# Thresholded attention and a gated MLP on one core: the tanh form of Gelu as one ScalarE function, with a new step order

## The chip, the cores and the metric

The kernel runs on one core of a Trainium2 chip, as one program. The metric is the device time of one execution in microseconds. Three runs of the kernel before gave 970.08, 971.67 and 973.45 us, so its median is 971.67 us. The engines are named as the profile names them: PE (TensorE), PEld (its weight loads), DVE (VectorE), ACT (ScalarE), POOL (GpSimd), SP (SyncE, which issues all DMAs here).

## The reference

Attention over 8 batches, 8 heads, 576 positions and head size 64, with a threshold below each row's maximum, and then a gated MLP over the concatenated heads:

```python
scores = scale * (q @ k.T)
keep = scores >= max(scores, axis=-1) - tau
attn = where(keep, exp(scores - max), 0); attn /= sum(attn) + 1e-9
x = heads_side_by_side(attn @ v)              # (8, 576, 512)
h = x @ w_in                                  # (8, 576, 1024)
h = 0.5 * h * (1 + tanh(c * (h + 0.044715 * h**3)))
u, v = h[..., :512], h[..., 512:]
v_n = (v - mean(v)) / sqrt(var(v) + 1e-6) * g_ln
gated = u * (w_sg @ v_n + b_sg[:, None])
out = x + gated @ w_out
```

The line with tanh is the one that the change touches.

## The kernel before, in words

**The attention part** (`attention`, lines 429 to 834) works on 32 pairs of heads. Each pair has nine tiles of 128 rows by 576 columns of scores. A tile goes through a fixed chain: PE makes the scores in PSUM (step `s`, line 558; line 533 for the first four pairs), DVE takes the negated row maximum (`nm`, line 567), POOL makes the threshold (`thr`, line 573), ACT takes the exponential from PSUM with the maximum as bias (`exp`, line 594), and DVE selects against the threshold, multiplies and sums (`stt`, line 601). Then the tile is turned. From the fifth pair on, tiles of both heads go out to DRAM and back by DMA (`move`, line 609, and `fetch`, line 618) and are turned in blocks by DVE (`turn32`, line 625); the rest is transposed on PE and copied out by ACT (lines 738 and 753). PE multiplies with the values (line 764), DVE scales (line 773), and ACT and POOL split the result into a rounded part `xh` and a remainder `xl`. The q and k of a pair are loaded, split and placed by further DMAs; these stand on lines 453 to 500.

**The MLP part** (`moe`, lines 874 to 1090) works on one batch at a time, between the attention tiles of the next batch, and on the last batch alone. Per batch there are five `v` units (four of 128 rows by 512 columns and one of 64 rows, whose accumulator is first folded into the tile `vt`), eight `u` units (128 by 288 in the first seven batches, 128 by 256 or 320 in the last), eight `y` units (the gate) and eight `o` units (the output). Products of all units are issued at line 866 in pieces of at most four matmuls. Each of the 13 `v` and `u` units of a batch ends with `gelu2` (line 838), which puts four steps into the plan:

- `msq`, line 845, ACT: Square of the accumulator into a buffer `gt`, scaled;
- `stt1`, line 852, DVE: (buffer + c) times the accumulator, back into the buffer;
- `tanh`, line 854, ACT: Tanh of the buffer, in place;
- `stt2`, line 849, DVE: (buffer + 1) times the accumulator, into the unit's own tile.

The accumulator stays in its PSUM bank through all four. The result is twice the Gelu, and later steps allow for that: the variance of `v` is normalised with 4e-6 in place of 1e-6 (line 946), and the gate multiplies by 0.5 (`mg`, line 1016). After a `v` unit follow DVE's statistics (lines 939 and 942), POOL's variance, power and shift (lines 946 to 954), ACT's normalisation (line 958), and the gain and the split into two parts (lines 961 to 976, POOL and ACT).

**What sets the order.** Every step is put into a plan of 5584 entries. A table, `ORDER`, is a permutation of the plan that is stored compressed; `issue` calls the steps in that order, and each engine's queue is then worked through in that order. A second table, `FIRST_BANKS`, names the PSUM bank of each request. SP issues all 1062 DMAs in the order of their steps.

Of the kernel before, what the change touches and what calls it, by code (L numbers as in the profile page):

```python
# [14 lines left out]
F32 = mybir.dt.float32  # L15
# [3 lines left out]
ALU = mybir.AluOpType  # L19
# [3 lines left out]
P = 128  # L23
# [6 lines left out]
GELU_C = 0.7978845608028654  # L30
GELU_A = 0.044715
# [40 lines left out]
    "Q1K)KJP+id|vru7<#@HhSsQ!r0;>%;RoHM2GQtq49^7D-65{9^H4Y7Vo>Pts#`$*o^)(U6i&Wya~Rs$tsV@`0Ozuv=<iiQk6TgDzw+SRnidN>GZ^|{ME"
    "nMrs{0zI0j$?Nw{UsR^14*lwbbz$xUvAY9?g@=5;{o}ci{BN@(-`@jrX67`{9R0FPwxIb|(D%^+CuuGSyx&G3U<TqJl1V_JQqq)V##QT3`M_!K?Ojcjw"
    "tRFT$w5$=ajAmAPjPf3SCv*7g22)q(MXaq*lxiNewj8oWf$*qVA=Qy1cbk%rylJJz;XdX$*cmSjr3DqWg|t1QVuOGH@YUIOsh`bCRE7O9=`hw=vtzImr"
    "S`kTCilcFC*%hoCUK3q5%7^hk0r9mh8s{`MJ@A&dfnSJGz0G}^eajtWuTWk!lYE%9gctjdLByc_0m;OryZ?BR0@&1`Ga#{f3mHfBDj9G8G2A9QNpKY)#"
    "(Y_78nm*egz@%U>N6mltRKHjNo1Xyl!ruD^S{7L_<AvWy(E5%aBvu|AQQ5<}YSUF%yPb$TW*h$rz{-y|xOwX%ThF`dNX-bed*vq@)05YNE!W`c0$96Xu"
    "bh!<<@M(BB;YF|;f){R{NO=(Vn2YBlExvEdguz_)#32bwEIrJcix{JGx7$V)FvI(ZoLdwlc4xg>U~RSS2G_7^)u&BI0pqE76SY+Bne7SM(HmFcd2!ZD~"
    "*MMHx~BsJrNdBWjvpOuy07xH3r;qM63K&Evoc_GF^k4f6&FRCOh|3lFC;to|3DF=yhQEbx52ALr5y9iL%s3H`a>*ApI7qm8_G_yN#7q(bjnD|0d)Q05h"
    "$<AgB6gSa?{(@RFUSVU|udV`UPUaQ5+Zgjx>j{CsQhJ<h-dTY}GtsrRIVSqs0aY3+GaXV>2AU*t||1^!kK98d&Hu>HoT+Y8gJccfLTqaMbO{#lxMq?Rm"
    "t_)c^)R)0)N<)7W^Az$p3zPA5mNaPy~SD<;wT`9=#Ku+$1gr=Z#p;EBk?4O61#Q<JBtqm_6C0-ba75yJ{>cAg+Njfv-u;j|f-#EP!2qlk`p8V~^h#k+J"  # L80
    "h2f_Fq8cHfF<=kCB)nn({4(WE$JPW>_sdd;yB!4VFSMqi(ir>NNVt^RPrMh&N8Hyq%R4>BOmnv1Xb$cIE?#`cv^yWxtp+~iwdte4r?dzlzGlGDF?5oPI"
    "0uk!*4g(#x4RkAr5EkFA@OCe?o%JywO>xVBs<RZEpX#CZV0FmU!aXU*ymzw(zfY%q$6fM(fX<3sW|zzs2u_M(SKZc<>QZknq^plHzm;fx(h@z7@mO-SX"
    "BU#Pez{r2!8~viNz2VmNyj6@-O-PnOeDem95*JaHBDM9#p`D3(0(0Z-?x>Q0W9|n(a{}4~5QW<#T`^J}LXu<JaA`(zL=@{jXuEyeSO$9aEhTqokFG4m<"
    "X~G3=;TDl3O`Fwa<N<W<*uyZ8^5o6=DhL;;i~PeuHEh_XX=^2{uKu5A*Jcw5-AImb&wOjt_z3_4tf_0jO|YFGz+&3hugdw$#*Pax}(3Hx(e){W3CU%qn"
    "tBjbhd1AnyRX?1v*J?rHE`pA;irOmf?8a*Iz(ziB<I8&lG>v<hn>r;<Tt|)Z>xoB_Z`3I6#n|3-Ihxt`L(plS?XdfC4r={(S^ZUfY+sTC|Y+CqX=JC?o"
    "+AvYLn)E8v!gmu4Uw>rDi4KSRLw}8`afVsI(2^QrDvS9;N*N-p20S};TATJbj5txyw_rk5XYBvKJpn8G-1oh@6hs9Bl<*~8$K3C-PcGsOl5Ew(h<!l~d"
    "YbwG&0V`J*<`6`N-Zhpb@T6ag_9uw$49De4#BQYO*o=;Xp=X;al5-&fAY06&!6E{I7D%LO<wPqvZ4f+R+G1NL2uAQRc`#FSZGfAr3XNVyg_+`^zi$*yv"
    "Vb0@ZNbi|2WlnUJAiEfn7d=6b_A{Py`Om_1?Cq*WpVixt~>FM7|}ly#DIq6BVa39fI$nvCo87ZGJ5BAy{uL{Oy^a8}rE<^vFLH;9hK@gproa+>x6R*@U"
    "+acFC%9Hn)^(r1U&%2fWA8M$}=y0gWIEjrbGTV1Q<@<EEmRpiZU!5PG6lqtI}8s<3#v6l@Ku4~l(?msGq9clh}L-0X%o<hTIg_Dgy7KJYB2E8hO%d0_N"
# [53 lines left out]
def tile_threshold_attention_gated_mlp(  # L143
# [691 lines left out]

    xh_of, xl_of = {}, {}

    def gelu2(put, end, acc_of, tile_of, nm_):

        t, tag = {}, slot("gt", 2)  # L840

# [5 lines left out]
        def gate():  # L847
            t["h"] = tile_of()
            nc.vector.scalar_tensor_tensor(t["h"], t["tmp"], 1.0, t["acc"], ALU.add, ALU.mult)  # L849
# [317 lines left out]
```

## Time and profile before

| | |
|---|---|
| median of three runs | 971.67 us |
| the profiled execution | 971.18 us, of which the span from first to last instruction is 969.4 us |
| granted TensorE clock, mean | 0.993 |
| PE, DVE, ACT, POOL busy | 889.2, 856.8, 560.1, 563.9 us |
| DMA queue 1, share of 16 engines over the span | 76.0% (212.40 MB) |
| ACT table loads | 1 |

Busy time is the time in which an instruction of the engine runs. Matmuls are pipelined and their ends are modelled, so a busy PE need not be a PE at its peak: a 128x288 matmul is shown as about 0.30 us while the next may start 0.13 us after it. The first 95 us hold the weights and the first pairs, the stretch from 95 to 865 us runs attention and MLP side by side, and from about 865 us on the last batch's MLP is alone.

### The profile page before, as it was taken

What the parts mean: (1) busy time and instruction counts of PE and PEld (TensorE: products, weight loads), DVE (VectorE), ACT (ScalarE), POOL (GpSimd) and SP (SyncE); (2) the same over time, 40 slices, a digit from 0 to 9 for tenths busy, and PEclk for the clock granted to TensorE, in tenths of its full rate; (3) what the DMA queues carried; (4) which work ended last, traced back from release to release, by engine and by line L of the source; (5) the groups of instructions that cost most, each with busy time, mean ns of one, the idle gap of its engine ahead of it and who ended that gap; (6) DMA issues with size and microseconds to landing.
All of it is one profiled execution on the core that took longest, in us unless ns stands there. A gap on an engine that the chain in (4) does not pass through costs nothing. (4 is left out here: it accounts for less than half of the span.)

```text
span 969.4 us, 18918 instructions
## 1 busy us (share of the span) xinstructions
PE 889.2 (92%) x5958; PEld 728.3 (75%) x5958; DVE 856.8 (88%) x1623; ACT 560.1 (58%) x1179; POOL 563.9 (58%) x997
## 2 busy tenths in 40 slices
PE   8999999889799898999889998999989999799998
PEld 4656777766688777987768777787778777598897
DVE  8999999999998899999999899998999899976541
ACT  6897764546654566544665456554565545554562
POOL 5765655546644566536754557646575456565287
PEclk9999999999999999999999999999999999999999
DMA  6533889999899897899878988899888898764001
GB/s 239 172 110 87 225 227 260 273 281 283 221 271 263 230 289 210 257 279 267 250 232 243 274 250 252 224 266 267 259 238 244 247 272 259 205 191 119 14 1 62
DMA packets 205388, 213.61 MB, mean 220 GB/s; under 512 B 22132, under 2 KB 141159, under 8 KB 205288
## 3 DMA queue, kind: packets, MB, share of 16 engines
q1 hardware_dynamic: 205288, 212.40, 76.0%
q8 instruction: 47, 0.77, 0.3%
q14 instruction: 53, 0.43, 0.1%
HBM read 103.03 MB, written 66.18 MB: 175 GB/s over the span
## 5 line engine op out<-in xcount | busy, mean ns | idle before, releaser
L594 ACT ACTIVATE p<-all_banks,nm 128x576 f32<-128x576 f32 x256 | 186.4, 740 | 160.6 <-DVE nm L567 142.3
L625 DVE STREAM_TRANSPOSE pt<-m 128x512 f32<-128x512 f32 x216 | 244.5, 1141 | 10.6 <-DMA m<-d 10.1
L567 DVE TENSOR_REDUCE nm<-all_banks 128x1 f32<-128x576 f32 x288 | 207.5, 746 | 20.8 <-PE all_banks L558 14.5
L601 DVE SCALAR_TENSOR_TENSOR p<-all_banks,nm,p 128x576 f32<-128x576 f32 x256 | 203.9, 807 | 12.5 <-ACT p L594 5.6
L558 PE MATMUL all_banks<-ks,qst 128*128 128x288 f32 x560 | 161.5, 320 | 23.9 <-DVE p L601 9.5
L573 POOL TENSOR_TENSOR nm<-columns,nm 128x1 f32<-128x1 f32 x288 | 54.0, 193 | 209.1 <-DVE nm L567 179.3
L764 PE MATMUL all_banks<-pt,rv 128*64 128x320 f32 (+1 forms) x1024 | 139.8, 412 | 12.7 <-DVE pt L625 10.5
L558 PEld LDWEIGHTS all_banks<-ks,qst 128*128 128x128 f32 x560 | 103.5, 191 | 47.1 <-DVE p L601 19.7
L558 PE MATMUL all_banks<-kl,qz 128*128 128x288 f32 x448 | 125.3, 296 | 1.8 <-POOL kl L466 1.7
L764 PEld LDWEIGHTS all_banks<-pt,rv 128*64 128x64 f32 x1024 | 71.0, 136 | 63.0 <-issue 9.9
L866 PE MATMUL all_banks<-wsh,z 128*128 128x288 f32 (+2 forms) x512 | 114.4, 299 | 1.4 <-DVE uu L1016 0.9
L866 PEld LDWEIGHTS all_banks<-wsh,z 128*128 128x128 f32 x512 | 85.1, 188 | 3.5 <-DVE uu L1016 1.3
L558 PEld LDWEIGHTS all_banks<-kl,qz 128*128 128x128 f32 x448 | 84.8, 189 | 3.0 <-POOL kl L466 2.9
L866 PE MATMUL all_banks<-xh,wih 128*128 128x288 f32 (+2 forms) x256 | 78.1, 307 | 7.0 <-ACT tt L753 3.0
L866 PE MATMUL all_banks<-gh,woh 128*128 128x288 f32 (+2 forms) x256 | 76.5, 302 | 1.7 <-DVE p L601 1.3
L866 PE MATMUL all_banks<-xl,wih 128*128 128x288 f32 (+2 forms) x256 | 77.2, 303 | 0.0
L866 PE MATMUL all_banks<-xh,wil 128*128 128x288 f32 (+2 forms) x256 | 76.5, 300 | 0.0
L866 PE MATMUL all_banks<-gh,wol 128*128 128x288 f32 (+2 forms) x256 | 75.5, 298 | 0.0
L866 PE MATMUL all_banks<-wsl,z 128*128 128x288 f32 (+2 forms) x256 | 75.3, 297 | 0.0
L866 PE MATMUL all_banks<-gl,woh 128*128 128x288 f32 (+1 forms) x240 | 71.7, 301 | 0.1
L866 PE MATMUL all_banks<-wih,xh 128*128 128x512 f32 x160 | 65.3, 410 | 2.7 <-DVE pm L601 2.1
L264 PE MATMUL all_banks<-ident_r,p 128*128 128x128 f32 x288 | 57.7, 284 | 10.2 <-DVE p L601 7.4
(146 smaller groups left out, 2138.0 us busy)
## 6 DMA issues: line engine op xcount, KB each, us to landing
d<-p SPq DMA_DIRECT2D x216, 256.0 KB
m<-d SPq DMA_DIRECT2D x216, 256.0 KB
rk<-in_kT SPq DMA_DIRECT2D x32, 320.0 KB
rv<-in_vP SPq DMA_DIRECT2D x32, 320.0 KB
ks<-khi SPq DMA_DIRECT2D x56, 160.0 KB
rq<-in_qT SPq DMA_DIRECT2D x31, 288.0 KB
qz<-qhi SPq DMA_DIRECT2D x56, 144.0 KB
qst<-rq SPq DMA_DIRECT2D x56, 144.0 KB
```

The costliest lines, as they stand in the source:

```text
L264: nc.tensor.transpose(out, x, ident_r.bitcast(F32))
L558: nc.tensor.matmul(sc[:, a, 0:HALF], w, x, start=(j == 0), stop=(j == len(terms) - 1))
L567: nc.vector.tensor_reduce(nmax, st["s", h, i][:, :, 0:HALF], AX.XY, ALU.max, negate=True)
L573: nc.gpsimd.tensor_tensor(thr, toff, st["nm", h, i], ALU.subtract)
L594: nc.scalar.activation(target(h, i), st["s", h, i][:, :, 0:HALF], AF.Exp, bias=st["nm", h, i])
L601: nc.vector.scalar_tensor_tensor(dst, st["s", h, i][:, :, 0:HALF], st["thr", h, i], dst, ALU.is_ge, ALU.mult, accum_out=st["l"][:, c:c + 1])
L625: nc.vector.transpose(unit(h, a)[:, :, j * P:(j + 1) * P].rearrange("p c (j a) -> p a c j", j=Q), st["m", h, i].rearrange("p (a k c) -> p ...
L764: nc.tensor.matmul(acc[h * D:(h + 1) * D, 0:w], st["v"][:, o:o + D], unit(h, a)[:, kt, 0:w] if kt < NM else tail_unit(a)[:, 0:w], start=(k ...
L866: nc.tensor.matmul(st["acc"], *term(j), start=(j == 0), stop=(j == n - 1))
```

## The change

`gelu2` with its four steps is replaced by `gelu` with one: ACT applies the function `Gelu_apprx_tanh` to the accumulator (or to `vt`) and writes the unit's tile. The buffers `gt` and `gtu` go. As the result is now the Gelu itself, the variance gets 1e-6 and the gate is a plain product.

```diff
-    def gelu2(put, end, acc_of, tile_of, nm_):
...
-            nc.scalar.activation(t["tmp"], t["acc"], AF.Square, scale=(GELU_C * GELU_A) ** 0.5)
...
-            nc.vector.scalar_tensor_tensor(t["h"], t["tmp"], 1.0, t["acc"], ALU.add, ALU.mult)
...
-        put("msq", end, square)
-        put("stt1", end, lambda: nc.vector.scalar_tensor_tensor(
-            t["tmp"], t["tmp"], GELU_C, t["acc"], ALU.add, ALU.mult))
-        put("tanh", end, lambda: nc.scalar.activation(t["tmp"], t["tmp"], AF.Tanh))
-        put("stt2", end, gate)
+    def gelu(put, end, acc_of, tile_of):
+        put("gelu", end, lambda: nc.scalar.activation(tile_of(), acc_of(), AF.Gelu_apprx_tanh))
...
-            gelu2(put, end, acc, new, f"{b}_{i}")
+            gelu(put, end, acc, new)
...
-                nc.gpsimd.tensor_scalar(t[:, 0:1], t[:, 7:8], 1.0, 4e-6, ALU.mult, ALU.add)
+                nc.gpsimd.tensor_scalar(t[:, 0:1], t[:, 7:8], 1.0, 1e-6, ALU.mult, ALU.add)
...
-            gelu2(put, time + spread, acc, new, f"u{b}_{p}_{d}")
+            gelu(put, time + spread, acc, new)
...
-                nc.vector.scalar_tensor_tensor(g, acc(), 0.5, g, ALU.mult, ALU.mult)
+                nc.vector.tensor_tensor(g, acc(), g, ALU.mult)
```

`ORDER` and `FIRST_BANKS` are new as a whole. The new table has 5272 entries. Decoded and laid over the plan, with the four steps of each unit replaced by one, it shows this:

- The stages stay where they were. When 72, 108, 144, 180, 216, 252 and 288 exponentials have been issued, both orders have issued 13, 25, 39, 52, 65, 78 and 91 of the units' Tanh or Gelu steps. The last 13 units of the 104 come after the last exponential in both.
- Steps that both orders share moved little: counted over the shared steps, nine in ten stand between 36 places earlier and 34 later, and the median is one place. This holds for SP's DMA steps as well, of which none is added or removed.
- On ACT's queue the 288 exponentials and the 104 Gelu steps form 84 runs of one function, so the function changes 83 times between the two. (Exponentials and Tanh steps formed 112 runs in the old order.) The last change is the one ahead of the last 13 Gelu steps.
- Between a tile's `nm` and its `stt`, DVE has a median of two other steps in both orders, and a mean of 2.75 in the old and 2.73 in the new. In the new order 69 of the 288 tiles have a change of function between their `nm` and their `stt`, and in 41 of them it is directly ahead of the tile's own exponential.

## Rows read from the trace of the kernel before

**Rows 1.** The page: busy time, share of the span and instructions of each engine.

```profile
PE 889.2 (92%) x5958; PEld 728.3 (75%) x5958; DVE 856.8 (88%) x1623; ACT 560.1 (58%) x1179; POOL 563.9 (58%) x997
```

**Rows 2.** Windows: stretch, PE, PEld, DVE, ACT, POOL busy (instructions), clock, DMA share, GB/s.

```profile
0.00:95.00 95.00, 86.74 (x540) 54.31 (x541) 87.73 (x204) 77.04 (x168) 59.98 (x122) 1.00 0.48 154
95.00:865.00 770.00, 703.74 (x4719) 584.19 (x4719) 719.87 (x1324) 433.83 (x902) 442.25 (x782) 0.99 0.88 250
865.00:969.00 104.00, 98.71 (x702) 89.85 (x700) 49.15 (x98) 49.25 (x110) 61.66 (x94) 1.00 0.20 59
```

**Rows 3.** Waits, whole span: who waited for whom, us in total, times, longest.

```profile
ACT p L594 <- DVE nm L567: 142.3, 106, 4.2
...
PEld all_banks L558 <- DVE p L601: 19.7, 31, 2.0
...
DVE uu L849 <- ACT gtu L854: 12.4, 10, 5.8
DVE pt L625 <- DMA m<-d: 10.1, 14, 2.1
...
DVE p L601 <- ACT p L594: 5.6, 15, 1.4
```

**Rows 4.** Windows, line 852 alone: stretch, DVE busy (instructions), clock, DMA.

```profile
95.00:865.00 770.00, 47.14 (x88) 0.99 0.88 250
```

**Rows 5.** Windows, line 849 alone: DVE busy.

```profile
95.00:865.00 770.00, 49.56 (x88) 0.99 0.88 250
```

**Rows 6.** Windows, line 854 alone: ACT busy.

```profile
95.00:865.00 770.00, 44.60 (x88) 0.99 0.88 250
```

**Rows 7.** Timeline of DVE near 118 us: start, us, engine, line, operation, tiles, shapes.

```profile
117.83 0.64 DVE L852 SCALAR_TENSOR_TENSOR gt<-gt,all_banks 128x512 f32<-128x512 f32 x1
118.39 0.41 DVE L355 TENSOR_TENSOR room<-all_banks,w 128x256 f32<-128x256 f32 x1
118.73 0.43 DVE L852 SCALAR_TENSOR_TENSOR gtu<-gtu,all_banks 128x288 f32<-128x288 f32 x1
119.09 0.20 DVE L652 RECIPROCAL ir<-l 128x9 f32<-128x9 f32 x1
```

**Rows 8.** Groups by shape: busy us, mean ns | idle before, releasers.

```profile
L594 ACT ACTIVATE p<-all_banks,nm 128x576 f32<-128x576 f32 x256 | 186.4, 740 | 160.6 <-DVE nm L567 142.3 <-DMA d<-p 5.3 <-issue 3.6
...
L845 ACT ACTIVATE gtu<-all_banks 128x288 f32<-128x288 f32 x56 | 22.5, 405 | 15.2 <-PE all_banks L866 11.6 <-DVE vv L849 3.2
...
L845 ACT ACTIVATE gt<-all_banks 128x512 f32<-128x512 f32 x32 | 18.8, 590 | 10.0 <-PE all_banks L866 10.0
...
L773 DVE TENSOR_TENSOR ir<-all_banks,ir 128x256 f32<-128x256 f32 x32 | 13.3, 416 | 1.7 <-PE all_banks L764 0.9 <-DMA d<-p 0.8
...
L1016 DVE SCALAR_TENSOR_TENSOR uu<-all_banks,uu 128x256 f32<-128x256 f32 x4 | 1.5, 415 | 0.8 <-PE all_banks L866 0.8
...
L307 ACT ACT_TABLE_LOAD x1 | 1.3, 1283 | 0.7 <-PEq L1148 0.7
```

**Rows 9.** Timeline of ACT, the first 10 us; in brackets the idle time before.

```profile
0.72 1.28 ACT L307 ACT_TABLE_LOAD   x1 [0.72 <-PEq L1148]
6.61 0.66 ACT L307 ACTIVATE room<-w 128x512 f32<-128x512 f32 x1 [4.61 <-DMA w<-in_w_in]
```

**Rows 10.** Windows with the columns of rows 2: the busiest 50 and 100 us of DMA.

```profile
195.00:245.00 50.00, 43.83 (x273) 32.05 (x273) 47.74 (x87) 28.65 (x56) 29.02 (x54) 1.00 0.98 283
200.00:300.00 100.00, 88.17 (x577) 70.02 (x576) 95.15 (x177) 56.96 (x117) 53.54 (x98) 0.98 0.91 261
```

**Rows 11.** The chain that ended last, 918 to 950 us: start, us, what.

```profile
923.41 0.53 ACT gt L854
923.96 0.70 DVE vv L849
...
942.23 0.37 ACT gtu L854
...
945.46 0.49 DVE uu L849
```

More of the change, by code (lines that the diff above doesn't have):

```diff
@@ new lines @@
+    "c-mcf2S60py8nD5J2SfrECZ`7EFc0_#Mn)OU5T0~DfSqQ#+DdM@?v6%S4|;RZ~l2t@6%|aMxsW&=0?$Iutj5wQ9x-Ty-8hQ*)~f#@08gE|FF!SIp-_C@"
+    "ArMD!Eqdi@Gtpr2&r%EoAdOdP8o00(@<OFg=r$z-N6j7VUIof*8v?I6<|MVKh^@=2M7@U;3k3&4;(71`a)Qr_I3cGBORO<KK{kVsR1&qhS0%6AUz$#1%"
+    "6?!I8Pu<1rH(>7r{aCVIv)C7}zob=0c5$yfV+Y3y5dZ>Yz$Qrk#vav-FRnp?MgjUrdKZLjkEVa%_<OQFY>-qm(eBR69fox7(><8hZzL80wnS4%K#tCve"
+    "6OeNYd?s3)})6-%qHO>a|)CLZ-RPLJDGW}3M4v*9rHRvfdh6@UBL^mNQd<gvKkh7jj<O`3SzhP-t}O{$fmM>eX&#I3-_$OGv)giYxgbyn~eC>`L4Tdam"
+    "%lP?UzhFBB3q5u#z#7dL2DK6?;&viCb9CT2X@DvsfkY_}ymWc#X!$TA!C5HUikS7L?dG$chBgP&g7Hml6(x#?}rAkjmDMIF#$k-?aT{-h=;8r`2=&-k}"
@@ new lines @@
+    "JfwOjFmcT>y97Q<j|VU5vQhXpMgl_K3C-#4IyG5X&F<+#dOI<!BZSi+Jrj*ZY2(yF(%C!L4D8L$0?=Wb*qApRYCKffyP(itDv5|=om~x9hhGqt)=|GCR"
+    "6FTa4Rx+coT}t8#;FcEsZ-}L($P0NwP{xsbgBT2nGBFNwV-1(sKRv6?tS4@Q7Y`Qrt+Y(GXbLE;ldL<!Rj&WT~_TXkBI5m)p&>lq#7q3M321bIQme1bu"
+    "Qv~)PYnVNG%CMBLSqPfzud?AT!D2Iy2XG*{3Mj2dTcWF+`wKT#O_{v3QIiMkgX6IJ7EC9c2jXX&q`%cBaG<uO`f!rOus+JhcS5gK2U|i(5p3JiX;Zp11"
+    "?)97Miz`$3$8#-v3KVuCasT04_+c;-7+r1pscs-q>s9Ov;!MM)pFrdF4hwmb_c9w)L|>dmt;B5%SOsYJrlhy5|Ks8K3|O>oFTgTN0~L!NBl5ybk5XQG8"
+    "T4<T9y=VgQ8U_C^OQ>kJfVqZ&C9iGss1yxxMp2eqS795laq|(7L&>s4ccK}g7m<)yMq&A#V7xzewgUWlhLxRSsb#&ppOA%?AGc|$CITnzd$Wx_=lSoM3"
@@ new lines @@
+    "qNPm|BQ>Vh0Pb`=aeU!eI$0_SM;s?H#v~_u<+P42ry><tms68kd7k`howP&kk(guZlfhuwWrj$KJxd`C(5YsL4m&(GA~`V_VwuJ!Iq^H`!^WK+I<=gW4"
+    "bWG~$$7KqK}NMb`v`@_If(}H7B3>U$+tx1NF2nF)**5DgE(wJLWFOu#yOcIjx=#Eg+$<ZTv901KG$XM@|GV4z=A^5AGWP!=*bX5P9{QCouuLPt^+Cu)C"
+    "K$E7ziiDND$&CVx63b<KQ}X1(i3ar*LS<SgvzNRcVu4s$pt~(n+I~*elB{)g;N`Xdpy~lE}Dss$>#CYTQn*4YfE>m%!BI(OwQYJ*#z>)yw0@8xf7r=@s"
+    "-GOj&fEnZsC?I7X$H3B~~ii=3XEs9kJhl)U+HVILkMCFD}`>q6{Hbb5}No+nKP))zU>g}Ph=I8JnVZwMj{oS<^4BBEMiPQ<E9By@6O=k)fZlKx;*c+5q"
+    "_M52ZPy6C9rQppx+Ay5g9eds%4#qabU56A#wn%D?O%wU@?sv=T%tc9DjlLkc{xI~5>iJszdiA<YQU5X65%TrjQ%M%L~>RgA&0Aew#@zNe@8H?e5${hj7"
@@ new lines @@
+    "LQ%zt0+V4RlQwdR2r=?V90+k<D3ooH1fr@?n=~-wJu9hjDD{LJ>P|)8nF|_z*9)P?Vb|j+@&qEP<w;3IE(R5&q)reENu>NC!i!qU)STe*B4XwUE6k7g!"
+    "b*EMSLZ6sDvi7fG*Ws7VkvQXueW%JQ;?b$BzB&|T`aqt!g%no)oGU%8|e_3KMy;CLVhVQ!6hgJJnE8q^+&*NIV8}E;X3clNL0v>fMZc8IHV9WtWRM|^c"
+    "VYJW?hU|1sfyd)QW%~ir`ZD#j;36#-6yBGzFxP2JNMQ$%tolCZ@dU7F19QO$nAIqXI#OIuUiA76im}1+ME}kG)aXWSDrR0=S8Xlr9H#)eFPoDYhr>vV<"
+    "3fap1v8Ls!Ej@hdFrY6xW1vp*|r8)7lA>QDracV>lS;UP+57cc^g*?V?SOH^=c6vUG5fvmP!I246S5PkE=d80)Pxj^yJS8u*KMJ*?R5Ty`i)r>I{bc7D"
+    "N5i4dd3Z$;Zf*Y~SYZNb!oXVa?;WUhr&a|t!!M_@}h8fhjDH0A_V&d$TQ#4eGg~ae8BBUDU6m>Fi8st`|qPMCvZu}wk$Txl=Skz@iLqupd>7awe8tFqC"
@@ new lines @@
+    "`b0#V3{ju>i+$K6P`Yg5p1f0U)ERm4{>RCUNGNWBqUKmMZlv*43JZxMAl~SNb<?s|RG@f>U_o@sQ8~gHZ6Sg7AcC0$st9hih}BLSIq}MTQynryB|IxC4"
+    "PGULSmY=N-Y<+D>(Mm2)r=u3q-s5J1AbyQde`wMj;^Tl#`i=Kb-jF`C-l%0!(H!bT-PJj|9_F>o|xRI%Lzd(##;a|>JI7#gCP`b_65QpBR94Q&-k4dp5"
+    "x)Pe$qKXXiThFurBdpUnmOC<)>a0#vR=lb|ZD_S+Q?%)WZ;HdiJ7j-M-*jsO!+XeB8ckj*c$9!S`+}kEk#}fLt>18rUVivQM+1gNMO_f4ic0jD(Oh2S4"
+    "N&9!yXvfx!)e6|_M*1i%R+js^)Dq2s}$9T|^B9}CDaWgP=ScXG~EeQRTIdq;V&*2k@Db@{g$9H7{0f?U&Tp$P<it?2eGG}V~Iihplvw)sDNp+w&UGA7p"
+    "bvSze4M>jM_w-xt^%%~q)+S<|&^7z33ji9OP0I9{__n|AyZ4lj}0q)Mo_kR>5cHDwUfM`=;P9i`v*sSf*<u_kx39`VsdG4lbkmw5s=Sl4#l$(SDVdFsa"
@@ new lines @@
+    "`-F#aMo6AlGckGc`6+4W;EkR06c}Gq85Uf7=oz`76^ftff2E($D)`^*)giihU0_Yl;7oHg2(1R^Rbw6BAGF{jv{qvgDY!**{`n5clKg>A>NvL0Cv`?@Z"
+    "Lnj`nHoRa^LG;hcC8X>1BC`Srk}oY^{zKv_6P4R-Cx+dpkHlcMM7gu90(QALvRptE`K8wT^|nqpy^R}U`fB%qF0)r#&UFFtI_)Tz6Zw^w8cTe+GlTmEf"
+    "~7jW0Soawr|?BwR>}$;GZSvcr<j?u50c{_+dUM!!Cw_)e8Qff!+Z|*vVHV&(iKvzODMI`|j(SZx5#(Se$U1umzJ~*@pntA^FofN_z3U26*Sn-9mPp3GM"
+    "(aJhbo-2p4BKo0p}ERpHR14v56jmNjvINWMQ{qyVKy&OYvyHX9G5B=JRup3Qpmcv4CO3~GnRpIX!8YB^NOevU_9K>ecb+rQX2z2APAa0SMj(_lgExh2&"
+    "<22VA;hs}Kb!PhwrPnRDXElmPDwB`gf+kgIcw)xwSw&iGD+OvZ*Vb!%AzrHkZ(ZS$F()?dA3i0ja&AXiM?^>0Sl5{$6u=dt7{*bXf38oY~WnFw~UJ9hZ"
@@ L119 @@
[L119 to L122 removed]
+    "c-l3S+XBNd2tw5u{r^86hjb6?S}%Z@L{#^kj?9Wv6J2L2IwR{Sv2~({hvKWm>?k!<(04Ox&*=$rr$XPViJVF$yY8egz+Gj`R2}nutdMR_tb)_R)qf>#u"
@@ L123 @@
+    "yutZ<^dkeXqY7}&PbAYD0<9@Y+;wx3uFQo6RJ}nf@|IcV2C^9VUnOVj3E15Acd%~Ixbk34AsS~*ND9RJ%Uj@Xk5n~PT*BOPpTaDPXrQ|;SNOMwxrFT)P"
+    "QA4i%Dmsv!u&&oJpJ@E88bNr?G^>V(uP4PRKVUid|heAX+%yuG{n%FAGCxVL**POt0}2hmVf>>SQVwN|}0c*1G=^gQbUd$jX)paT#Hj#L<vk`SO9|sWt"
+    "T5C64>Nh1c`sT@Tp~a0<h2>6MkcVE8OfPak#qPc#Q#7(t?ZfO6v7mZy3<V;>^YWB09o3RARU;|S!Nv-cav7sA?d?sHsSx(R~yNE>(WyFir(E7)ZCPW=F"
+    "0$_f7"
 )
```

136 lines of the change are left out of this document (44 added, 92 removed).

## The prediction

> **What bounds the kernel now.** I read the page's busy times first [rows 1]: PE 92%, DVE 88%, ACT and POOL 58%. That average hides three stages, so the windows come next [rows 2]. From 0 to 95 us hardly anything of the change exists. From 95 to 865 us DVE is busy 719.9 of 770 us (93.5%), ACT 433.8 (56%), and the DMA engines have a mean share of 0.88. From 865 us on DVE is busy 49 of 104 us and PE 98.7: the last batch's MLP is PE's, with POOL beside it. Then the waits [rows 3] say who sets the pace in the long stage: ACT waits 142.3 us, 106 times, for DVE's maximum, PE's weight loads wait 19.7 us for DVE's select, while DVE waits only 5.6 us for ACT's exponential. So DVE leads, ACT follows with slack, and the stage from 95 to 865 us is where the change is decided. A PE of 91% there is no proof of a PE at its limit, since a matmul is shown longer than the distance to the next.
>
> The sum is made against the profiled execution's 971.18 us (span 969.4, 1.8 around it), which stands 0.5 us under the median of 971.67. A measurement of this kernel can tell about 0.3%, or 2.9 us, from no change.
>
> **Removed from DVE: the two products.** In the long stage line 852 is busy 47.1 us and line 849 49.6 us, 88 instructions each [rows 4, 5], together 96.7. An instruction of DVE overlaps the next a little: 117.83 to 118.39 is 0.56 us for one shown as 0.64, and 118.73 to 119.09 is 0.36 for one of 0.43 [rows 7], so about 0.08 us of each comes back. 176 x 0.08 = 14, and the path gets shorter by 96.7 - 14 = 83 us. DVE's work in the stage falls from 720 to 637 us. The bounds are 75 (an overlap of 0.12 us) and 97 (none). Waits inside the four-step chain go as well, such as the 12.4 us of line 849 for Tanh [rows 3], much of them in the last stage; what is late next is the statistics of `v`, which wait for the Gelu itself, and the gate product, which waits for PE as before.
>
> **Removed from and added to ACT.** Tanh goes: 44.6 us in the stage [rows 6]. Square becomes Gelu on the same operands, PSUM to SBUF: I take Square's 405 ns for 128x288 and 590 ns for 128x512 [rows 8], so nothing. A Gelu that took less would change nothing, as ACT does not lead. The bound above is the exponential's 740 ns for 128x576, the longest row of this kind; that would add at most 104 x 0.3 = 31 us to an engine with 336 us of idle in the stage, and hides in its waits for `nm`.
>
> **Table loads.** The trace has one load, of 1283 ns [rows 8], for Abs, Exp, Square, Tanh, Copy and Identity together. No row shows whether Gelu is served by the same load. The lower bound is none more. The upper is one at every change between exponential and Gelu in the new order: 83, of which 82 fall before the last stage, 82 x 1.283 = 105 us of ACT work. I take the upper end. ACT in the stage is then 433.8 - 44.6 + 105 = 494 us, still under DVE's 637. How much comes out on DVE is the real question. The one load of the trace ran at 0.72 us, while its own instruction waited for a DMA until 6.61 us [rows 9]: a load does not wait for the data of the instruction behind it. ACT's waits for `nm` average 142.3/106 = 1.34 us [rows 3], about one load, so a load ahead of an exponential falls largely into a wait that is there anyway. Its cover is DVE's other work between `nm` and `stt`, a median of two steps. Where that is gone, up to 1.28 us stands in DVE's way, and behind it every later exponential on ACT's queue. I let a quarter show, 82 x 0.32 = 26 us, as new idle of DVE.
>
> Here the Trainium skill speaks against the change. "ScalarE: Activation LUTs", section "Table sets: the hidden batching unit", says that tables are loaded as sets, lists exp with tanh in one set, gives gelu a set of its own, calls gelu_apprx_tanh separate from that, and tells to batch calls by set; "What ACT_TABLE_LOAD costs" prices a switch at about 2.66 us with its drain. No run here shows that drain; by that price ACT's work would be 433.8 - 44.6 + 82 x 2.66 = 607 us, an estimate from that page, close to DVE's 637.
>
> **Gate, variance, PSUM, order.** The gate as a plain product costs what it did: DVE's plain product of 128x256 from PSUM takes 416 ns, the three-operand one 415 [rows 8]. The variance's constant is free. A unit's PSUM bank is given back after one instruction in place of four on two engines; I count nothing for it, and that can only help PE run ahead. All other steps, the DMA steps of SP's queue included, are the same in number and mostly moved by no more than some tens of places out of 5272, with the stages as before, so I price the move at nothing. Its cover is that DVE and SP still get the same work per tile, and if a move does hurt, it shows as a wait for `fetch` or `nm`.
>
> **DMA and PE as the next limit.** The stage's transfers are unchanged: 0.88 x 770 = 678 us of mean busy time. The busiest 50 us reached a share of 0.98 and the busiest 100 us 0.91 [rows 10]. Over a whole stage I take 0.95: 678/0.95 = 713 us. DVE would then be busy 637/713 = 89%, with 76 us idle in place of 50. Those 26 us more are the ones that I gave the loads, so the two limits say the same. The stage gains 770 - 713 = 57 us.
>
> **The last stage.** It is PE's and POOL's, but the chain that ended last goes through Tanh and the product of a `v` unit at 923.41 to 924.66 us, 1.25 us, and through the last `u` units from 942.23 to 945.95 us, 3.7 us [rows 11]. Two Gelus of some 0.4 us replace the latter. I count 1.25 + 3.7 - 0.8 = 4 us gained; the bounds are 0, where POOL's work on `v` is late anyway, and 5. Its one load comes with the first of the 13 and lies ahead of this chain. The first 95 us: nothing.
>
> **Sum, case A:** 971.2 - 57 - 4 = 910 us. Chance 0.45 for 898 to 927.
>
> **The rivals.**
>
> - *Case D, the loads cost DVE nothing.* DVE keeps its 50 us of idle in the stage: 637 + 50 = 687, and 971.2 - 83 - 4 = 884. For it: ACT's slack of 336 us. Against it: DMA would stand at 678/687 = 0.99 throughout, seen for no more than 50 us. Chance 0.15.
> - *Case C, something else holds the pace.* If DMA cannot go above its best 100 us, 0.91, the stage takes 678/0.91 = 745 us, and the time is 971.2 - 25 - 4 = 942; PE's products, which queue behind the select, would look the same. For it: the shares are near that already. Against it: DVE waits only 10.1 us, 14 times, for a fetched block, and PE's waits are for DVE [rows 3]. Chance 0.29, from 927 to 970.
> - *Case B, slower: loads in the chain from maximum to select.* The place is ACT's queue between `nm` and `stt`, where 69 tiles have a change of function. If no load is covered, all 82 are DVE idle: the stage takes 770 - 83 + 105 = 792 us, and the time is 971.2 + 22 - 4 = 989. It decides from the point where a load shows as (83 + 4)/82 = 1.06 us on DVE, four fifths of its own length. For it: DVE has only two other steps between the two. Against it: the waits of ACT for `nm`, and rows 9. This is the batching rule of the Trainium skill's page on activation tables as a mechanism of this kernel; at that page's price, two fifths of each switch would be enough to lose. Chance 0.11.
> - *The change does not do what it says*, a Gelu with no load at all: the same as case D or C, since only ACT's slack would grow.
>
> **How the numbers follow.** The predicted time is case A's, 910. A, D and nearly all of C lie between 882 and 955, which leaves out B and C's far end, under 2 in 10; the bounds of DVE's saving (75 to 97) and of Gelu move the time by less than that. Faster by over 0.3%: A, D and C up to 968, 0.86. Within 0.3%: 0.03. Slower: 0.11, case B.
>
> **What would show it.** Right: DVE busy near 765 us in the whole span, no rows for the two products, 84 ACT table loads of 1283 ns each, ACT busy near 610 us, the stage about 713 us long with a DMA share of about 0.95, DVE waiting for the exponential by some 20 to 30 us where it waited 5.6. Wrong towards B: DVE waits for `exp` by 100 us or more, behind loads. Towards C: waits of DVE for fetched blocks and of SP for earlier DMAs grow, with ACT idle. Towards D: DVE still 93% busy in the stage. A last stage longer than 104 us would be outside all of them.

## The result and the profile after

The changed kernel takes 943.9 us (median of four runs, 942.56 to 946.53), against 971.45 us for the kernel before on the same chip. The ratio is 0.9718, with a 95% interval of 0.9689 to 0.9748: 27.5 us less. The forecast was 910 us, 61 less. The kernel got faster, but by less than half of that, and the time lies near rival C's 942 us.

The page's busy times of the changed kernel, the line that answers to [rows 1]:

```profile
PE 876.3 (93%) x5958; PEld 726.5 (77%) x5958; DVE 765.4 (81%) x1415; ACT 619.4 (66%) x1158; POOL 559.5 (59%) x997
```

The windows of the changed kernel, with the columns of [rows 2]. The long stage now ends at about 840 us:

```profile
0.00:95.00 95.00, 85.55 (x534) 53.74 (x535) 85.38 (x195) 77.62 (x169) 58.93 (x123) 1.00 0.52 158
95.00:840.00 745.00, 691.62 (x4718) 581.92 (x4717) 645.24 (x1154) 494.22 (x891) 437.68 (x780) 0.99 0.89 257
840.00:943.00 103.00, 99.16 (x711) 90.85 (x709) 34.79 (x69) 47.53 (x100) 62.92 (x95) 1.00 0.23 68
```

DVE lost 91 us of work, 856.8 to 765.4, of which 75 in the long stage. But the stage got shorter by only 25 us, 770 to 745, so DVE's idle time in it doubled, from 50 to 100 us. The share of the DMA engines hardly moved: 0.88 before, 0.89 now.

The groups of ACT in the changed kernel, loads and Gelu (busy us, mean ns | idle before, who ended it), against the square and the load of [rows 8]:

```profile
L832 ACT ACT_TABLE_LOAD x42 | 53.9, 1283 | 8.9 <-PE all_banks L843 7.5 <-DVE vt L897 0.8
L587 ACT ACT_TABLE_LOAD x41 | 52.6, 1283 | 0.8
...
L832 ACT ACTIVATE uu<-all_banks 128x288 f32<-128x288 f32 x56 | 22.3, 405 | 6.5 <-PE all_banks L843 5.4 <-POOL gl L1013 0.9
...
L832 ACT ACTIVATE vv<-all_banks 128x512 f32<-128x512 f32 x32 | 19.0, 596 | 8.7 <-PE all_banks L843 8.4
```

There are 83 loads more, one at each change of function, and a Gelu costs what the Square did. The waits of the changed kernel (us in total, times, longest), against [rows 3]; lines 618, 560, 916, 993 and 594 are the turn, the maximum, the statistics of `v`, the gate and the select:

```profile
ACT p L587 <- DVE nm L560: 87.4, 78, 3.9
DVE pt L618 <- DMA m<-d: 32.5, 47, 2.9
...
DVE nm L560 <- PE all_banks L551: 27.0, 37, 1.6
...
DVE bn L916 <- ACT vv L832: 22.1, 17, 5.3
...
DVE uu L993 <- PE all_banks L843: 13.6, 11, 7.7
...
DVE p L594 <- ACT p L587: 10.6, 23, 1.4
```

The largest new wait of DVE is for the tile fetched back from DRAM: 32.5 us in 47 waits, where it was 10.1 in 14. It is not the only one. Of the 50 us that DVE is idle more in the long stage, this wait makes 22 (10.1 to 32.0); the wait for the scores makes 14 (8.3 to 22.1), the one for the Gelu ahead of the statistics, which is new, 10, and the one for the exponential 7 (1.4 to 8.8). In the timeline of DVE in the changed kernel (start, us, what, and in brackets the idle before) such waits look like this:

```profile
504.58 1.15 DVE L618 STREAM_TRANSPOSE pt<-m 128x512 f32<-128x512 f32 x1 [0.80 <-DMA m<-d]
...
511.35 1.14 DVE L618 STREAM_TRANSPOSE pt<-m 128x512 f32<-128x512 f32 x1 [2.92 <-DMA m<-d]
```

ACT's timeline a moment earlier shows a load ahead of an exponential:

```profile
510.59 1.28 ACT L587 ACT_TABLE_LOAD   x1
513.14 2.29 ACT L587 ACTIVATE p<-all_banks,nm 128x576 f32<-128x576 f32 x3 [1.27 <-DVE nm L560]
```

The load ended at 511.87 and ACT still waited 1.27 us for the maximum: that load was hidden in the wait. A load ahead of a Gelu is not always hidden like this. Of the 42, 8 came only after ACT had waited for the data of the Gelu itself, 8.3 of the 8.9 us of idle time in the first row of the groups above, and the load then stood behind that wait:

```profile
149.48 1.28 ACT L832 ACT_TABLE_LOAD   x1 [2.99 <-PE all_banks L843]
150.78 0.41 ACT L832 ACTIVATE uu<-all_banks 128x288 f32<-128x288 f32 x1
```

So what [rows 9] showed of one load, that it does not wait for the data of the instruction behind it, held for the 41 loads ahead of an exponential, none of which waited over 0.1 us, and not for those 8.

### The profile page after: what moved, and what is told of

It reads as the page before. It is cut to its first block, busy times and chain, and to the rows that moved or that the text cites. A ratio compares the mean times of both kernels' runs of the same rounds, so it can differ in the third digit from the quotient of the medians.

```text
span 943.2 us, 18697 instructions
## 1 busy us (share of the span) xinstructions
PE 876.3 (93%) x5958; PEld 726.5 (77%) x5958; DVE 765.4 (81%) x1415; ACT 619.4 (66%) x1158; POOL 559.5 (59%) x997
## 4 chain that ended last, share of the span: by engine, by line
PE 39%; DMA 21%; DVE 13%; ACT 11%; issue 7%; POOL 5%; SPq 4%; POOLq 0%; DVEq 0%; ACTq 0%
PE all_banks L843 17%; PE all_banks L757 8%; PE all_banks L551 7%; DMA d<-p 6%; DMA m<-d 5%; ACT p L587 3%; DVE nm L560 3%; DVE p L594 3%; DVE pt L618 3%; PE all_banks L257 3%; DMA ks<-khi 2%; DMA out_T<-ot 2%; PE all_banks L526 1%; DMA ir<-ld 1%; ACT L587 1%
## 5 line engine op out<-in xcount | busy, mean ns | idle before, releaser
L618 DVE STREAM_TRANSPOSE pt<-m 128x512 f32<-128x512 f32 x216 | 245.2, 1142 | 33.3 <-DMA m<-d 32.5
L587 ACT ACTIVATE p<-all_banks,nm 128x576 f32<-128x576 f32 x256 | 185.2, 741 | 109.8 <-DVE nm L560 87.4
L560 DVE TENSOR_REDUCE nm<-all_banks 128x1 f32<-128x576 f32 x288 | 208.4, 747 | 32.5 <-PE all_banks L551 27.0
L594 DVE SCALAR_TENSOR_TENSOR p<-all_banks,nm,p 128x576 f32<-128x576 f32 x256 | 202.9, 807 | 24.3 <-ACT p L587 10.6
L843 PE MATMUL all_banks<-wil,xh 128*128 128x512 f32 x160 | 63.0, 394 | 0.0
```

The costliest lines, as they stand in the source:

```text
L560: nc.vector.tensor_reduce(nmax, st["s", h, i][:, :, 0:HALF], AX.XY, ALU.max, negate=True)
L587: nc.scalar.activation(target(h, i), st["s", h, i][:, :, 0:HALF], AF.Exp, bias=st["nm", h, i])
L594: nc.vector.scalar_tensor_tensor(dst, st["s", h, i][:, :, 0:HALF], st["thr", h, i], dst, ALU.is_ge, ALU.mult, accum_out=st["l"][:, c:c + 1])
L618: nc.vector.transpose(unit(h, a)[:, :, j * P:(j + 1) * P].rearrange("p c (j a) -> p a c j", j=Q), st["m", h, i].rearrange("p (a k c) -> p ...
L843: nc.tensor.matmul(st["acc"], *term(j), start=(j == 0), stop=(j == n - 1))
```

## The experiments

Four theories stood at the start. **D**: the DMA engines set the new pace. **L**: the loads eat the gain. **R**: the round trip through DRAM does, by its buffers or its length. **O**: the fixed order does. **P** (PE) and **S** (SP's queue) came later. Ratios are to the kernel before, measured beside it on the same chip; one point of ratio is 9.7 us. The kernels marked with a star leave out or replace part of the computation.

| run | ratio | 95% interval |
|---|---|---|
| changed kernel | 0.9718 | 0.9689 to 0.9748 |
| e1, no loads * | 0.9647 | 0.9623 to 0.9671 |
| e2, Gelu in the old order | 1.0344 | 1.0312 to 1.0376 |
| e3, four buffers | 0.9670 | 0.9644 to 0.9696 |
| e4, 14.7 MB more | 1.0045 | 1.0026 to 1.0064 |
| e5, as many small DMAs more | 0.9768 | 0.9719 to 0.9818 |
| e6, half of the round trip's bytes * | 0.9430 | 0.9395 to 0.9465 |
| e7, the same in the kernel before * | 0.9869 | 0.9836 to 0.9902 |
| e8, a third less of the MLP's products * | 0.9669 | 0.9599 to 0.9738 |
| e9, e2 without loads * | 0.9846 | 0.9822 to 0.9870 |
| e10, e6 without loads * | 0.9278 | 0.9259 to 0.9297 |
| e11, placement on POOL | 0.9807 | 0.9783 to 0.9830 |
| e11, placement on DVE | 0.9764 | 0.9740 to 0.9787 |
| e12, fewer bytes elsewhere * | 0.9619 | 0.9582 to 0.9657 |
| e13, changed kernel again | 0.9735 | 0.9702 to 0.9769 |
| e14, four buffers again | 0.9699 | 0.9666 to 0.9733 |
| e15, placement on ACT | 0.9714 | 0.9677 to 0.9751 |

### The loads

```diff
-        put("gelu", end, lambda: nc.scalar.activation(tile_of(), acc_of(), AF.Gelu_apprx_tanh))
+        put("gelu", end, lambda: nc.scalar.activation(tile_of(), acc_of(), AF.Tanh))
```

> The changed kernel with Tanh in place of the Gelu function, in the same order: Tanh shares its table load with the exponential, so all but one of the 84 loads should go and nothing else changes in the work (the unit's tile then holds tanh of the accumulator and not its Gelu). Theory L (the 83 added loads eat the gain, by standing in ACT's queue): 925 us or less, ACT busy down by 83 x 1.283 = 106 us. Theory D (the DMA engines are the limit, case C): within 5 us of 943.9. Theory R (the round trip through DRAM, out, back and turned, is what DVE waits for, by its latency and its two buffers): within 8 us of 943.9, a little below. Theory O (the fixed order with PE, DVE and ACT taking turns): 930 to 942.

Measured: 0.9647, or 7 us less than the changed kernel (0.71 points; 3 to 11 us by the two intervals). One load was left, and ACT was busy 514.4 us, 105 less. 83 loads that occupy ACT for 106 us are worth 7 us of time, 0.08 us each. L falls as the main cause. Where the loads hide can be read from ACT's wait for the maximum, which is 122.6 us without them and 87.4 with them in the same order:

```profile
ACT p L587 <- DVE nm L560: 122.6, 105, 4.5
```

The 41 loads ahead of an exponential are 52.6 us, and 35 us of that wait are gone.

### The order

The merged step was put where the old order had the fourth of its steps, and the old bank table came with the old order:

```diff
-ORDER = (the new table)
+ORDER = (the old table, with "msq", "stt1" and "tanh" left out and "stt2" standing for "gelu")
```

> The Gelu function in the old order and with the old bank table, Gelu in the place of the fourth of its old steps: the change without its new order. The functions on ACT then change 111 times, so 112 loads. Theory L: 28 more loads than the new order at the same price, so 10 us or more above 943.9. Theory D: the transfers are the limit in either order, 940 to 950. Theory R: 945 to 960. Theory O (the order is laid out for the engines' loads): 955 or more, most of the gain gone.

Measured: 1.0344, slower than the kernel before. The change without its new order, with the Gelu at this place, loses 3.4%; against it the new order and its bank table are worth 6.3 points, 61 us. The waits of e2 show where, 22.6 us of DVE for the exponential and 44.0 for the Gelu ahead of the statistics, against 10.6 and 22.1 in the changed kernel:

```profile
DVE bn L839 <- ACT vv L755: 44.0, 22, 4.6
...
DVE p L517 <- ACT p L510: 22.6, 33, 3.6
```

One rival stands untested here. The place of the fourth step is a late one: counted in steps that both orders share, the new order has the Gelu a median of 12 steps ahead of it, 4 behind the place of the old first step. The old order with the Gelu at that earlier place was not run, so how much of the 61 us a better place alone would give is open.

Taking the loads out of that kernel separates the two parts.

> e2_old_order with Tanh in place of the Gelu function: the merged step in the old order, without its 112 table loads (the tiles hold tanh of the accumulator). e2_old_order took 1.0344 of the kernel before, the new order 0.9718. If the loads make the difference (theory L, in an order that was not laid out for them): 0.985 or less of the kernel before, and most of e2's 61 us over the new order gone. If the sequence itself does (theory O): 1.015 or more.

Measured: 0.9846. The loads of the old order cost 5.0 points, 48 us or 0.43 us each, against 0.08 us each in the new one. So most of the new order's worth against this kernel, some 41 of 61 us, is that it hides loads; without any loads the sequence itself is worth 2.0 points (0.9846 to 0.9647), 19 us.

### Buffers

```diff
-ROOMS = 2
+ROOMS = 4
```

> The changed kernel with four buffers in place of two for the tiles fetched back from DRAM; the two freed buffers of the old chain make room. Order, bytes and work are the same; a fetch no longer waits for the turn of the tile two before it. Theory R: 935 us or less, with DVE's 32.5 us of waits for the fetched tile falling under 15 and SP's 27 us for the turn gone. Theory D: within 3 us of 943.9, since the same bytes go through the same engines. Theories L and O: within 4 us.

> e3_rooms4 once more, beside the changed kernel in the same call: if the four buffers are worth something, 3 to 6 us less than e13_changed_again; otherwise within 2 us.

Measured: 0.9670 the first time. Beside the changed kernel on one chip (e13, 0.9735) it was 0.9699, 2.5 us less by the medians, with overlapping intervals and between the two bounds. SP's 27 us of waiting for the turn ahead of a fetch went in e3, DVE's wait for the fetched tile stayed (31.0 us in e3, 32.5 before). The number of buffers is not it; no gain is shown.

> The changed kernel itself, to stand beside the others of this call on one chip: 0.972 of the kernel before under every theory.

### Bytes and issues

```diff
+                if name == "v" and n >= WHOLE_SCORES:
+                    for x in range(2):
+                        extra = mtmp.tile([P, FH], F32, tag=f"extra{x}", name=f"extra{n}_{x}")
+                        nc.sync.dma_start(extra, src[:, 0:FH])
```

> The changed kernel with two further loads of 256 KB per pair of heads from the fifth pair on (56 in all, 14.7 MB, into two otherwise unused tiles). At the 111 ns that a 2 KB packet takes on average in the changed kernel's trace, 56 x 128 packets over 16 engines are 50 us of DMA time. Theory D: the time grows by most of that, 980 us or more. Theories R, L and O: under 955; R nearer to that, as every transfer lands later.

e5 is the same with `extra[0:16, 0:16]` and `src[0:16, 0:16]`.

> As e4_more_dma, but each of the 56 further loads brings 1 KB (16 partitions of 64 bytes) in place of 256 KB: the same number of issues on SP's queue and almost no bytes. In e4_more_dma these loads cost 31.8 us by the ratios. Theory D (the time of the DMA engines): within 5 us of the changed kernel's 943.9. Theory S (SP's queue, which issues one DMA after the other at some 0.5 us each, 56 x 0.5 = 28 us): 965 or more.

Measured: e4 1.0045, 31.8 us over the changed kernel (3.27 points); e5 0.9768, 4.9 us over it, with an interval that touches the changed kernel's. Both expected bounds for e4 were missed, but between 955 and 980 it is nearer to D's. The issues alone are about a sixth of it by the medians, and at most a third by the intervals: S falls. The bytes themselves cost about 27 us of time. The estimate of 50 us for them is too large: by the traces (queue 1's share of the 16 engines times the span) e4 has 769 us of DMA time and e5 738, 31 us less. DVE's wait for the fetched tile in e4 rose to 55.6 us:

```profile
DVE pt L622 <- DMA m<-d: 55.6, 58, 2.3
```

Then the other way, half of the round trip:

```diff
-                nc.sync.dma_start(st["d", h, i].rearrange("g q c -> q g c"), ...)
+                k = P // Q // 2
+                nc.sync.dma_start(st["d", h, i][0:k].rearrange("g q c -> q g c"), ...)
...
-                st["m", h, i] = ppool.tile([P, MAIN], F32, tag=tag, name=f"m{n}_{h}_{i}")
-                nc.sync.dma_start(st["m", h, i], st["d", h, i].rearrange(...))
+                st["m", h, i] = kept[int(tag[1:])]
+                nc.sync.dma_start(st["m", h, i][0:k * Q], st["d", h, i][0:k].rearrange(...))
```

> The changed kernel with half of each tile in the round trip through DRAM (two of four blocks go out, 64 of 128 partitions come back, into two buffers that are set to zero once; DVE turns the whole buffer as before). Same number of DMAs, half of their bytes: 216 x 256 packets of 512 B at 28 ns and 216 x 64 of 2 KB at 111 ns less, over 16 engines 97 + 96 = 193 us of 735 of DMA time. Theory D: DMA falls under 0.75 of the stage and the time goes towards the 884 to 910 that the freed DVE allows. Theory O (the order of the queues): 930 to 944. Theory P (PE is the new limit): above 925.

> The kernel before with the same half round trip. Theory D with DVE leading before the change: at most 10 us under the kernel before. If the DMA engines already set the pace before: 25 us or more under it. The difference between what the half trip is worth in the two kernels is what the change has handed from DVE to the transfers.

Measured: 0.9430 in the changed kernel, 28 us less than it; 0.9869 in the kernel before, 12.7 us less. In e6 DVE's wait for the fetched tile, 32.5 us in the changed kernel, is all but gone:

```profile
DVE pt L623 <- DMA kept<-d: 4.2, 9, 1.0
```

The same cut is worth about twice as much after the change, so the change moved part of the limit to the transfers. The kernel before was not free of it: theory D, with DVE leading there, allowed 10 us at most, and the interval of the 12.7 just reaches that. The windows from the 73rd to the 253rd maximum, five batches in the steady part (columns of [rows 2]), of the kernel before, of the changed one, of e4 and of e6:

```profile
204.00:782.30 578.30, 529.04 (x3548) 439.78 (x3546) 539.10 (x987) 320.81 (x666) 328.37 (x578) 0.99 0.89 254
```

```profile
203.30:761.40 558.10, 519.51 (x3562) 440.04 (x3561) 483.35 (x856) 363.82 (x660) 328.14 (x580) 0.99 0.91 264
```

```profile
206.10:789.20 583.10, 526.75 (x3562) 442.75 (x3561) 483.42 (x857) 364.42 (x660) 329.02 (x582) 0.98 0.92 272
```

```profile
202.90:737.50 534.60, 511.46 (x3561) 435.53 (x3562) 479.90 (x857) 364.15 (x661) 327.73 (x580) 1.00 0.72 196
```

DVE has the same work in the last three, 480 to 483 us, and they last 583 us (e4), 558 (changed) and 535 (e6), in the order of their bytes. With more transfers the share went to 0.92, which e1 also had with the changed kernel's bytes; no kernel of this study held more over such a stretch.

Last, fewer bytes that have nothing to do with the round trip:

```diff
-                nc.sync.dma_start(st[name][:, :w], src)
+                c = w if n <= WHOLE_SCORES else P
+                nc.sync.dma_start(st[name][:, :c], src[:, 0:c])
...
+                if n > WHOLE_SCORES:
+                    rows = slice(h * D, h * D + 4)
```

> The changed kernel with fewer bytes outside the round trip and the same number of DMAs: from the sixth pair on, the load of v brings 128 of 640 columns (into a tile that is kept, so the rest stays from an earlier pair), and the two placements of q's rounded part into the single-head tiles bring 4 of 64 rows. 27 x 128 packets of 2560 B at 135 ns become packets of 512 B at 28 ns, 23 us over 16 engines, and 27 x 2 x 60 packets of 2304 B at 128 ns go, 26 us: 49 us less, the mirror of e4_more_dma. The round trip itself is untouched, no engine gets work. Theory D (total time of the DMA engines): 15 us or more less than the changed kernel in this call. Theory R2 (only the round trip's own length counts, and e6_half_trip shortened that): at most 8 us less.

Measured: 0.9619 beside 0.9735 for the changed kernel on the same chip, 11 us less, between the two bounds (the intervals leave 6 to 16 us, and so reach both). DVE's wait for the fetched tile was 23.3 us, against 29.0 in e13:

```profile
DVE pt L627 <- DMA m<-d: 23.3, 31, 1.9
```

So bytes outside the round trip count too, but less and less. By the traces, where the estimates had 50, 49 and 193: 31 us of DMA time more (e4 against e5) cost 27 us, 31 us less (e12 against e13) gave 11, and 167 us less (e6, in the round trip) gave 28. That fits a limit that is shared with others. So does the chain of work that ended last in the changed kernel, followed back over its whole span, which goes through PE more than through DMA:

```profile
PE 39%; DMA 21%; DVE 13%; ACT 11%; issue 7%; POOL 5%; SPq 4%; POOLq 0%; DVEq 0%; ACTq 0%
```

How much of e6's gain is the shorter round trip, and how much the lower load of the engines, these runs don't separate.

### What is left without both

> e6_half_trip with Tanh in place of Gelu: neither full transfers nor loads. e6 stood at 0.943 and e1 (no loads) 0.7 points under the changed kernel. If the two limits are independent: 0.935, about 908 us, near the predicted 910. If the loads were hidden behind the waits for transfers in e1 and come out once these are gone (theory L in second place): 0.925 or less. If something else holds it then: 0.940 or more.

Measured: 0.9278, 900.6 us. Without the loads e6 gains another 1.5 points, 15 us, where e1 gained 7: with the transfers out of the way, more of the loads comes out. With neither the kernel runs 43 us faster than the changed one, and its window of the same five batches reads:

```profile
199.40:723.90 524.50, 507.21 (x3562) 433.91 (x3563) 479.39 (x856) 293.42 (x604) 327.49 (x580) 1.00 0.72 200
```

DVE is still idle in 45 of 524 us, 8.6%; in the kernel before it was 6.8%. What holds this kernel was not tested. PE, busy in 96% of its span, is one candidate, and the fixed order another.

### PE

```diff
                 for j in range(lo, hi):
+                    if j % 3 == 1 and j < n - 1:
+                        continue
```

> The changed kernel without every third matmul of the MLP's products (the second of each three terms is left out, the first and the last of a sum stay), some 800 matmuls of 0.13 us or more, about 110 us of PE work of the 770 or so that it needs. Theory P (PE has become the limit): 925 us or less. Theory D: within 8 us of 943.9 outside the last stage, which is PE's and gets shorter by some 15 us, so 925 to 935 in all with all of it after 865 us; theory O: as D, with up to 10 us more in the long stage.

Measured: 0.9669, 4.8 us less than the changed kernel, with overlapping intervals. That is above what theories P and D gave and within theory O's range (up to 945). PE had 86 us less to do (790.6 us busy) and DVE's waits for the scores ahead of the maximum stayed at 24.6 us, where they had been 27.0. P falls for the changed kernel. The last stage did not shorten as expected either. The windows from the last maximum to the end of the changed kernel and of e8:

```profile
878.30:943.00 64.70, 60.86 (x417) 56.37 (x415) 11.44 (x26) 26.59 (x59) 41.02 (x60) 1.00 0.08 26
```

```profile
875.00:938.00 63.00, 48.47 (x299) 42.70 (x297) 11.51 (x26) 26.15 (x59) 40.67 (x60) 0.92 0.08 27
```

118 matmuls fewer took 1.7 us off the end, while the mean granted clock of this stretch fell from 1.00 to 0.92.

### A version with fewer transfers

The rows of q's rounded part stay on their partitions when they are put into the single-head tiles, so an engine can do it:

```diff
-                nc.sync.dma_start(qz[h][rows].bitcast(F32), st["qh"][rows, :S].bitcast(F32))
+                nc.gpsimd.tensor_scalar(qz[h][rows], st["qh"][rows, :S], 1.0, 0.0, ALU.mult, ALU.add)
```

(on DVE `nc.vector.tensor_scalar`, on ACT `nc.scalar.activation` with Copy; all with four buffers).

> A candidate that computes the reference: the changed kernel with four buffers for fetched tiles (as e3_rooms4), and with the two placements of q's rounded part into its single-head tiles, whose rows stay on their partitions, done by POOL in place of two DMAs of 144 KB per pair (56 issues and 8 MB less; at 128 ns per packet of 2304 B, 56 x 64 packets over 16 engines are 29 us of DMA time). POOL gets 56 x 0.77 = 43 us more of 560. Theory D: 925 to 935 us, since e4 showed that 50 us of DMA time are worth some 27 us. If POOL's queue, where each tile's threshold stands, is held up by the copy: 944 or more.

> As e11_place_on_pool, with the copies on DVE (56 of about 0.65 us, 36 us more of 765). Theory D: 930 to 940, the freed DMA time against DVE time of about the same size on an engine that is now 81% busy. If DVE still set the pace: 965 or more.

> The placement of q's rounded part by ACT, with four buffers: 56 copies of about 0.68 us less the overlap, 34 us of ACT work at 66%, against 29 us of DMA time. Theory D: 925 to 940, since ACT does not lead and POOL's queue (which held the copy up in e11_place_on_pool) is free again. If whatever engine does the copy waits for PE's last use of the tile ahead of it: 945 or more.

Measured: 0.9807, 0.9764 and 0.9714. DVE's waits for the fetched tile fell to 15.4, 10.3 and 9.9 us, as D wants it, and the time did not: all three lie above what D expected. In the waits of the version with POOL the time reappears on ACT, which may not overwrite q's rounded part before POOL has copied it (for the DMA in the changed kernel it waited 13.2 us):

```profile
ACT khi L454 <- POOL qz L473: 27.1, 16, 3.0
```

On DVE the copies put 32 us of work (797.2 against 765.4) on the engine that had just been relieved. On ACT the time stayed where it was: 0.9714, within the interval of the changed kernel, though queue 1 had 25 us of DMA time less than in e13 (703 against 728); what took the gain there was not found. None of the variants that compute the reference is shown to beat the changed kernel.

## Why the prediction was wrong

**The step that failed** is the one on DMA as the next limit: "Over a whole stage I take 0.95: 678/0.95 = 713 us". The share in the stage became 0.89, and the stage took 745 us, so it gained 25 us where the sum had 57. The 0.95 has no row behind it that is as long as the stage. [rows 10] and the prediction call 200 to 300 us the busiest 100 us, with 0.91, and that is a misreading: the stretch from 140 to 240 us had 0.96, and 0.91 is what the busiest 300 us held.

```profile
140.00:240.00 100.00, 91.27 (x609) 74.00 (x611) 94.69 (x173) 52.72 (x111) 53.22 (x97) 1.00 0.96 275
165.00:465.00 300.00, 272.38 (x1829) 224.88 (x1827) 279.69 (x508) 161.67 (x339) 164.56 (x297) 0.99 0.91 261
```

The longer the stretch of the kernel before, the lower the share: 0.98 in the 50 us of [rows 10], 0.96 in 100, 0.91 in 300, 0.88 in the 770 us of the stage. I took for the whole stage what only 100 us had shown. More load in e4 brought 0.92 over five batches.

That the transfers are part of what stands in DVE's way is shown by e4, e6 and e12: half the trip's bytes gave back 28 of the 34 us that were missing (e6), though such a cut was worth 13 us before the change as well (e7). That they are the whole of it is not shown: less DMA time elsewhere gave less (e12) or nothing (the placements), and with the transfers cut and no loads 17 us are still missing to case D.

**Rival C** came within 2 us, in part by luck. Its 942 rests on 678/0.91 = 745 us, with the 0.91 of the misread row; measured were 0.89 x 745 = 663 us of transfers in the stage, as part of them stood in the first and last stretch. At a share of 0.91 those 663 us would have given 729 us. What C had right is that something besides DVE holds the pace.

**Two limits that said the same.** The sum took 26 us for the loads and found the same 26 us in the transfers, and counted them once. Measured, the loads were worth 7 us and half the trip's bytes 28; that the two terms agreed was chance.

**DVE's removed work** was a little too large: 83 us in the stage, with bounds of 75 and 97. It was 75 (719.9 to 645.2), the lower bound; the overlap with the next instruction takes more than the two pairs of [rows 7] showed. Over the whole span the 208 instructions of the two lines are shown with 115.0 us, and DVE's busy time fell by 91.4, so 0.11 us of each had been overlap, where I took 0.08.

**The loads** came as the upper end had them: 83 more, 1283 ns each, ACT at 619.4 us busy where I had some 610. Case B, that they stand in the way, did not happen in the new order: they cost 7 us, not the 26 that I gave them, and mainly for the reason given, ACT's waits for the maximum (122.6 us without the loads and 87.4 with them, in the same order). With the transfers cut they cost 15 us (e10 against e6), which suggests that the waits for transfers hide a part of them.

The Trainium skill ("ScalarE: Activation LUTs", "What ACT_TABLE_LOAD costs") prices a switch at about 2.66 us with its drain. That did not show: in the changed kernel's trace the median gap was 18 ns ahead of a load and 12 ns behind it, so 1.31 us. The Trainium skill's rule to batch calls by set (the same page, "Table sets: the hidden batching unit") holds where the order does not cover the loads: in the old order (e2 against e9) they cost 48 us and made the change a loss. Case B is thus shown as a mechanism, but of another order.

**The order priced at nothing** was a second wrong step, though not one that shows in the sum, which took the loads in the new order. That steps moved by a median of one place said nothing of its worth: 61 us against the old order with the Gelu at its last step's place (e2).

**The gate, Gelu's own time and the start** held: the plain product of 128x288 took 441 ns where the three-operand one had 443, the Gelu 405 and 596 ns against the Square's 405 and 590 [rows 8], and the 73rd maximum came at 203.3 us, 0.7 earlier than before.

**The last stage**: 4 us forecast, 1.1 measured (66.0 to 64.9 us from the last maximum to the end). The Tanh and products on the old chain [rows 11] went; the chain of the changed kernel goes through POOL's work on `v` instead, which the lower bound of 0 had allowed for:

```profile
910.88 0.53 ACT vv L832
...
912.74 1.30 POOL z L951
...
915.84 1.29 POOL vv L938
```

**The others.** Case D (884 us) is not reached even with the transfers halved and no loads (900.6). Of the two signs that I named for C, one came: waits for fetched blocks tripled, while SP's waits for earlier DMAs hardly grew, 57 to 62 us over the span. Those for A came only in the counts, 84 loads and DVE at 765 us; the share stayed at 0.89, and DVE waited 10.6 us for the exponential, not 20 to 30.

## What to carry to other kernels

When work is taken from the leading engine, read what the next resource has held over stretches as long as the stage, and not over its best 50 or 100 us, and search all stretches before one is called the busiest. A function from another table set can be cheap if the engine that loads it waits anyway just there; whether it does is a property of the order, so a change of function and its order have to be judged together, as the same change lost 3.4% in the order made for its predecessor, with the new step at the place of the old last one. Waits that go away in one place (buffers, placements by an engine) are not time gained while the queues are in a fixed order: measure the time.

## What the runs showed of the hardware that was not expected

- A table load follows an activation after 18 ns and is followed by the next after 12 ns (medians of 83). In the trace:

```profile
504.02 0.74 ACT L454 ACTIVATE khi<-rk 128x640 fp32r<-128x640 f32 x1 [0.79 <-DMA qz<-qhi]
504.78 1.28 ACT L832 ACT_TABLE_LOAD   x1
506.08 0.41 ACT L832 ACTIVATE uu<-all_banks 128x288 f32<-128x288 f32 x1
```

- A load can run ahead of its activation's wait for data or behind it: 11 of the 41 loads ahead of an exponential ended while the maximum was still missing, by up to 3.2 us, and 8 of the 42 ahead of a Gelu began only after up to 2.99 us of waiting for the Gelu's data. What decides between the two is not shown.

- With fewer matmuls the mean granted clock was lower, 0.965 in e8 (0.953 to 0.973 in its four runs) against 0.989 in the changed kernel and 0.996 in e10, whose PE was the busiest of all (96% of the span). In e8 15% of the matmuls went and PE's busy time fell by 10%. In its last stage PE had waited 2.20 us until 903.28 and 2.00 us until 913.43, and behind each wait stands a stretch at the lower level of the clock, 1.2 of 2.4 GHz:

```profile
903.80:907.10 3.30, 3.30 (x17) 3.30 (x16) 0.86 (x2) 1.15 (x2) 0.95 (x3) 0.50 0.00 0
914.10:917.40 3.30, 3.30 (x15) 3.30 (x15) 1.75 (x4) 0.47 (x1) 1.82 (x3) 0.50 0.13 45
```
